# Adaptive layer norm, linear attention and SwiGLU on one core: key tiles in pairs, heads innermost, second-norm statistics by sums, and a new order

## The chip, the cores and the metric

The kernel runs on one core of one Trainium2 chip. The metric is the time of one execution on the device in microseconds (us). A core has five engines that run side by side, each through its own list of instructions in the order in which the program has them: TensorE (PE, matmuls, with its weight loads PEld beside them), VectorE (DVE), ScalarE (ACT), GpSimd (POOL) and SyncE (SP), which only issues transfers. An engine stops at an instruction whose semaphores have not been raised, and whatever stands behind it on that engine stops too.

## The reference

`x` is 2048 tokens of 512 numbers in bf16. The reference, cut to what matters:

```
mod = silu(c) @ w_mod                    # six vectors of 512: sa, ca, ga, sb, cb, gb
h   = layernorm(x) * (1 + ca) + sa
q, k, v = split(h @ wqkv)                # 32 heads of 16
phi(t) = concat(softmax(t @ w_phi), softmax(-(t @ w_phi)))    # 32 features a head
kv  = sum over tokens of phi(k) v^T ;  z = sum over tokens of phi(k)
o   = (phi(q) kv) / (phi(q) z + 1e-6)
x   = x + ga * (o @ wo)
h   = layernorm(x) * (1 + cb) + sb
out = x + gb * ((silu(h @ w_gate) * (h @ w_up)) @ w_down)     # 1376 hidden numbers
```

## The kernel before

The 2048 tokens are 16 tiles of 128, four to a chunk of x. The stages, with the lines of the profile:

- **Start.** silu(c) times w_mod gives the first norm's scale and shift `modA` (L473, L478). w_phi is spread into blocks `BD` (L499, L502) and folded into the key and query weights by transposes, matmuls and casts (L519, L523, L530, L533), so that a key tile comes out of PE as k times w_phi at once. The first norms of x run beside this.
- **Key tiles** (`k_tile`): four matmuls of 512 columns for k (L619) and four for v (L623); two exponentials on ACT, of the value and of its negative (L634); their sums over each head on DVE (`S`, L640); 1/S on ACT as exp(-ln S) (L644, L645); v times 1/S on DVE into `va` (L650), and 1/S itself as 32 more columns of `va` (L652 to L654); the second feature half scaled on POOL (L657). `kv_tile` adds phi(k) times va into the accumulator `kv_ps` (L663).
- **Query tiles** (`q_tile`): four matmuls (L686), two exponentials (L690), sums (L694), a reciprocal (L696), a ratio (L697), a scale (L701), and a transposing transfer into `pT`.
- **Attention** (`attend_tile`): eight short matmuls of pT with `KVZ` into `kv_ps` (L824). The program has one such bank, so the next tile's matmuls wait until DVE has read this one's: a reciprocal of the denominators (L827) and the product `o` (L828).
- **Projection and second norm** (`project`): o transposed, times wo (L857), added to x on DVE (L860), statistics on DVE (L348, L349), the reciprocal standard deviation on POOL (L359 to L362), the normalized tile on ACT, POOL or DVE, its transpose by a transfer, and scale and shift `modB` (L878 to L882).
- **Feed-forward**: gate and up (L909), silu on ACT (L916), the product on DVE or on ACT and POOL (L919, L923, L925), down (L987), the last sums (L993 to L1001) and the transfers out (L1007). The last tile's output leaves in three pieces, of 256, 128 and 128 columns.

What stands where on an engine is decided ahead of time. Each operation is recorded with `pl.op`, with one or more engines that could do it; `ORDER` is a table of numbers, one for each operation, which picks the engine and the order; `Plan.run` gives each operation a planned start from built-in costs, and the engines' lists are the operations sorted by it. Where the plan leaves PE idle in the first 90 us, `fill` puts matmuls of a tile of ones into the list (L1054), whose results nobody reads. They are meant to keep PE at work, and take the time of any matmul of their width. Such a matmul writes into `kv_ps` or into the bank that the next real matmul will write:

```
            elif late:
                dst = kv_ps[:, 0, :] if o.news[0].tag == "four" else one_ps[o.news[0].slot]
```

Of the kernel before, what the change touches and what calls it, by code (L numbers as in the profile page):

```python
# [14 lines left out]
P = 128  # L15
# [20 lines left out]
def fm_size(m):  # L36
# [53 lines left out]
class Buf:  # L90
# [14 lines left out]
    def free_at(self):  # L105
        if self.keep:
            return None
        t = 0.0
        for u in self.users:
            if u.end is None:  # L110
                return None
# [982 lines left out]
```

## Time and profile before

| | before |
|---|---|
| runs | 199.42, 199.49, 199.85 us (median 199.49) |
| span of the profiled execution | 197.6 us; of the same execution no other time is given |
| busy share PE, DVE, ACT, POOL | 98%, 71%, 56%, 60% |
| granted TensorE clock | 1.00 of full speed in every stretch |
| first key matmul, start of the last matmul | 12.74 us, 194.12 us |

The profile is one execution; its span runs from the first instruction to the last event, and the timed runs are 1.9 us longer at the median. Busy time is what an engine spends in instructions; the chain is the work that ended last, followed backwards from the end.

### The profile page before, as it was taken

The numbers are of one execution on the slowest core, as the hardware profiler recorded it, in microseconds if no ns is written. First come the engines' busy times: TensorE is split into PE (matmuls) and PEld (weight loads), VectorE is DVE, ScalarE is ACT, GpSimd is POOL, SyncE is SP. The second block draws the span as 40 slices with busy tenths as digits, with TensorE's granted clock in tenths as the row PEclk, the third lists the DMA queues.
The fourth block names the chain that finished last, engine by engine and source line by source line (L and its number), as shares of the span: only waits on it lengthen the run. The fifth ranks groups of instructions, "written<-read, shape, count | busy, mean of one in ns | idle before, by whom it ended". The sixth has DMA issues, their size and how long they took to land.

```text
span 197.6 us, 4084 instructions
## 1 busy us (share of the span) xinstructions
PE 192.9 (98%) x1495; PEld 108.4 (55%) x1495; DVE 139.9 (71%) x272; ACT 111.6 (56%) x252; POOL 119.5 (60%) x198
## 2 busy tenths in 40 slices
PE   7999999999999999999999999999999999999993
PEld 2765555555754776886575554454445444444452
DVE  5999999999999999989868689384122421181653
ACT  2699999999769982665263625435723411235200
POOL 1459999999996669656757979406761004065310
PEclk9999999999999999999999999999999999999999
DMA  6997994999928672835377515400340020100202
GB/s 210 370 373 116 168 316 162 213 181 389 324 53 170 117 138 42 157 65 102 77 113 135 109 36 87 100 0 0 80 98 25 0 63 17 56 15 27 80 29 79
DMA packets 51142, 24.17 MB, mean 122 GB/s; under 512 B 42449, under 2 KB 47922, under 8 KB 51122
## 3 DMA queue, kind: packets, MB, share of 16 engines
q1 hardware_dynamic: 50976, 23.88, 50.0%
q8 instruction: 11, 0.18, 0.3%
q14 instruction: 9, 0.07, 0.1%
q10 hardware_dynamic: 146, 0.03, 0.1%
HBM read 11.58 MB, written 2.10 MB: 69 GB/s over the span
## 4 chain that ended last, share of the span: by engine, by line
PE 98%; DVE 0%; issue 0%
PE one_ps L909 35%; PE one_ps L987 19%; PE one_ps L857 7%; PE one_ps L623 7%; PE one_ps L619 7%; PE one_ps L686 7%; PE kv_ps L1054 4%; PE one_ps L955 3%; PE kv_ps L663 2%; PE kv_ps L824 2%; PE one_ps L530 1%; PE one_ps L473 1%; PE one_ps L414 1%; PE one_ps L519 0%; PE one_ps L722 0%; DVE ones L296 0%
## 5 line engine op out<-in xcount | busy, mean ns | idle before, releaser
L909 PE MATMUL one_ps<-hT,wgu_sb 128*128 128x512 bf16 (+2 forms) x480 | 75.7, 308 | 0.0
L909 PEld LDWEIGHTS <-wgu_sb 128*128 128x128 bf16 x480 | 40.3, 98 | 27.7
L916 ACT ACTIVATE sg<-one_ps 128x512 bf16<-128x512 f32 (+1 forms) x41 | 23.7, 588 | 41.8 <-PE one_ps L909 29.9
L925 POOL TENSOR_TENSOR gu<-usb,sg 128x512 bf16<-128x512 bf16 x19 | 21.8, 1151 | 39.7 <-ACT usb L923 19.9
L987 PE MATMUL one_ps<-wd_sb,gu 128*128 128x512 bf16 (+1 forms) x160 | 37.7, 372 | 0.0
L919 DVE TENSOR_TENSOR gu<-one_ps,sg 128x512 bf16<-128x512 f32 (+1 forms) x22 | 14.3, 652 | 21.1 <-PE one_ps L909 19.0
L987 PEld LDWEIGHTS <-gu 128*128 128x128 bf16 x180 | 16.6, 98 | 16.7
L997 DVE TENSOR_TENSOR fg<-one_ps,gab 128x512 bf16<-128x512 f32 (+1 forms) x16 | 10.5, 669 | 19.6 <-PE one_ps L987 19.4
L348 DVE BATCH_NORM_STATS2 st<-x_c 128x6 f32<-128x512 bf16 x32 | 21.0, 679 | 0.1
L640 DVE TENSOR_REDUCE S<-e 128x64 f32<-128x1024 bf16 x16 | 19.1, 1207 | 0.2
L694 DVE TENSOR_REDUCE Sq<-eq 128x64 f32<-128x1024 bf16 x16 | 19.0, 1201 | 0.0
L923 ACT CAST usb<-one_ps 128x512 bf16<-128x512 f32 x19 | 11.3, 594 | 13.5 <-PE one_ps L909 13.2
L690 ACT ACTIVATE eq<-one_ps 128x512 bf16<-128x512 f32 x32 | 17.3, 644 | 2.2 <-PE one_ps L686 2.2
L634 ACT ACTIVATE e<-one_ps 128x512 bf16<-128x512 f32 x32 | 16.9, 600 | 0.0
L657 POOL TENSOR_TENSOR e<-e,S 128x512 bf16<-128x512 bf16 x16 | 16.8, 1056 | 0.1
L857 PE MATMUL one_ps<-wo_sb,oT 128*128 128x512 bf16 x64 | 16.1, 379 | 0.0
L623 PE MATMUL one_ps<-wv,hT 128*128 128x512 bf16 x64 | 16.1, 379 | 0.0
L619 PE MATMUL one_ps<-wk,hT 128*128 128x512 bf16 x64 | 15.8, 379 | 0.0
L686 PE MATMUL one_ps<-wq,hT 128*128 128x512 bf16 x64 | 15.8, 379 | 0.0
L701 POOL TENSOR_TENSOR eq<-eq,Rq 128x512 bf16<-128x512 bf16 x13 | 14.2, 1096 | 0.5
L860 DVE TENSOR_TENSOR x_c<-x_c,one_ps 128x512 bf16<-128x512 bf16 x16 | 10.6, 674 | 4.5 <-PE one_ps L857 4.4
L880 ACT ACTIVATE hT<-raw,modB 128x256 bf16<-128x256 bf16 x16 | 8.9, 594 | 8.1 <-DMA raw<-xn 8.1
(120 smaller groups left out, 279.8 us busy)
## 6 DMA issues: line engine op xcount, KB each, us to landing
wmod_sb<-in_w_mod_dram SPq DMA_DIRECT2D x2, 1024.0 KB, 8.5
out_dram<-ot SPq DMA_DIRECT2D x15, 128.0 KB, 2.0
x_c<-in_A_x_dram SPq DMA_DIRECT2D x3, 512.0 KB, 6.7
wgu_sb<-in_B_w_up_dram SPq DMA_DIRECT2D x1, 1376.0 KB, 10.2
wgu_sb<-in_B_w_gate_dram SPq DMA_DIRECT2D x1, 1376.0 KB, 13.1
wd_sb<-in_B_w_down_dram SPq DMA_DIRECT2D x1, 1280.0 KB, 6.8
wk<-in_A_wqkv_dram SPq DMA_DIRECT2D x1, 512.0 KB, 4.9
wmod_sb<-in_w_mod_dram SPq DMA_DIRECT2D x1, 512.0 KB, 5.3
```

The costliest lines, as they stand in the source:

```text
L348: pl.op("DVE", r=reads, w=[st6], us=0.6, fn=lambda: nc.vector.bn_stats(st6()[:], src))
L619: nc.tensor.matmul(pk()[:], lhsT=hT[c_i][k][:, cols], rhs=Wk2[:, k, :], start=(k == 0), stop=(k == KD - 1))
L623: nc.tensor.matmul(v()[:], lhsT=hT[c_i][k][:, cols], rhs=wv_sb[:, k, :], start=(k == 0), stop=(k == KD - 1))
L640: pl.op("DVE", r=[e], w=[Ss], us=1.13, fn=lambda: nc.vector.tensor_reduce(Ss()[:].rearrange("p g s h -> p (g s h)"), e()[:].rearrange("p g ...
L686: nc.tensor.matmul(pq()[:], lhsT=hT[c_i][k][:, cols], rhs=Wq2[:, k, :], start=(k == 0), stop=(k == KD - 1))
L690: pl.op("ACT", r=[pq, btab], w=[be[sg]], us=0.48, fn=lambda sg=sg: nc.scalar.activation(eq[:, :, sg].rearrange("p g h f -> p g (h f)"), pq ...
L694: pl.op("DVE", r=be, w=[Sq], us=1.13, fn=lambda: nc.vector.tensor_reduce(Sq()[:].rearrange("p g s h -> p (g s h)"), eq[:].rearrange("p g s ...
L857: nc.tensor.matmul(a()[:], lhsT=oT()[:, j0 + j, :], rhs=wo_sb[:, j, :], start=(j == 0), stop=(j == KD - 1))
L909: nc.tensor.matmul(ps_()[0:fsz, q * n:(q + 1) * n], lhsT=wgu_sb[:, k, i, m * P:m * P + fsz], rhs=h2[k], start=(k == 0), stop=(k == KD - 1))
L916: pl.op("ACT", r=[g, btab], w=[sg], us=0.08 + 0.41 * L / CW, fn=lambda: nc.scalar.activation(sg()[0:fsz, 0:L], g()[0:fsz, 0:L], ACT.Silu))
L925: pl.op("POOL", r=[usb, sg], w=[gu], us=0.17 + 0.98 * L / CW, fn=lambda: nc.gpsimd.tensor_tensor(gu()[0:fsz, 0:L], usb()[0:fsz, 0:L], sg() ...
L987: nc.tensor.matmul(fp()[:], lhsT=b()[0:fsz, c0:c0 + P], rhs=wd_[0:fsz, m, wcs], start=(m == 0), stop=(m == FM - 1))
```

## The change

- **Key tiles in pairs.** The sums of two tiles go into one tile `S`; 1/S of both is one Ln and one Exp of 128 columns on ACT, and the Exp writes straight into the extra columns of `va`, which now holds both tiles. The copies L652 to L654 are gone, the ratio is made once for a pair (`rho`), and kv is accumulated two tiles at a time.
- **Heads innermost.** Features are stored as [16 features][4 heads] and not [4 heads][16 features]. A reduction then reads its 16 numbers with a step of four elements, and a scale is read as a contiguous run of four.
- **Second norm of tiles 2 to 15.** The addition to x becomes an instruction that also sums its output (after's L921), and ACT squares x with a sum (L924); six small operations on POOL for a pair (`rstd_sums`) replace three for each tile and 14 of the 32 BN_STATS with their BN_AGGR.
- **Start.** The silu of c is Exp, Ln, Exp on ACT and one product on DVE; w_phi's block is first copied out and then multiplied in two halves; the four casts of the folded key weights are all on ACT (two were on DVE).
- **End.** Of the last tile's three pieces the middle one leaves on ACT's queue, and no longer the last one.
- **The plan.** A released buffer is picked by its last use, GpSimd and certain DVE operations exclude each other by intervals, one transfer constant is 0.85 and not 1.1, and `ORDER` is another table.

```diff
@@ k_tile, k_pair
-        pl.op([("DVE", 0.46, lambda: nc.vector.reciprocal(R()[:], Ss()[:])), ("ACT", 0.47, fr)], r=[Ss], w=[R])
...
+    def k_pair(i0):
+        Ss, parts = bS[i0]
+        R = sb("kph", "R", [P, 2, G, 8], FP32)
+        va = Buf("va", lambda slot: va_t[slot])
+        def fr():
+            nc.scalar.activation(R()[:], Ss()[:], ACT.Ln)
+            nc.scalar.activation(va()[:, :, :, HG:HG + 8], R()[:], ACT.Exp, scale=-1.0)
...
-        pl.op("DVE", r=[e], w=[Ss], us=1.13, fn=lambda: nc.vector.tensor_reduce(
-            Ss()[:].rearrange("p g s h -> p (g s h)"), e()[:].rearrange("p g s h f -> p (g s h) f"), axis=AX.X, op=ALU.add))
+            Ss()[:, y].rearrange("p g (s h) -> p (g s) h", s=2), e()[:].rearrange("p g s f h -> p (g s) h f"), axis=AX.X, op=ALU.add))
...
@@ project, prepare
+        pl.op("DVE", r=[a, bx[n]], w=[bx[n], sums[r]] + ([mv] if r == 0 else []), us=0.68, fn=lambda: nc.vector.scalar_tensor_tensor(
+            xs, in0=a()[:], scalar=1.0, in1=xs, op0=ALU.mult, op1=ALU.add, accum_out=mv()[:, r, 0:1]))
+        pl.op("ACT", r=[bx[n], mv, sums[r]], w=[sums[r]] + xn2[2], us=0.62, fn=lambda: nc.scalar.activation(
+            xn2[1](), xs, ACT.Square, scale=D ** -0.5, accum_out=mv()[:, r, 1:2]))
...
@@ ffn_down
-            on_act = c1 == D and h == 1
+            on_act = c0 == D // 2 and c1 < D
```

The real matmuls are the same in number and width, 427,380 columns in all (the widths in PE's two lists added up). The fill matmuls are 27 with 11,780 columns before and 30 with 13,809 after. Ahead of the first key matmul they have 11,025 columns before and 12,075 after; 512 columns of real transposes that stood ahead of it now stand behind it.

What PE has at the first key matmuls (`one_ps` are PSUM banks, `hT` the normalized and transposed x, `xn` the normalized x). Before:

```order
L414 MATMUL one_ps_75<-ident_b,xn_326 128x128
...
L1054 MATMUL kv_ps<-ones 128x184
L619 LDWEIGHTS hT_0_144
L619 MATMUL one_ps_78<-wk,hT_0_144 128x512
L619 MATMUL one_ps_78<-wk,hT_1_145 128x512
L619 MATMUL one_ps_78<-wk,hT_2_146 128x512
```

After:

```order
L1122 MATMUL kv_ps<-ones 128x385
L652 MATMUL one_ps_76<-wk,hT_0_143 128x512
L652 MATMUL one_ps_76<-wk,hT_1_144 128x512
L440 MATMUL one_ps_75<-ident_b,xn_326 128x128
...
L652 MATMUL one_ps_78<-wk,hT_0_143 128x512
L652 MATMUL one_ps_78<-wk,hT_1_144 128x512
L1122 MATMUL kv_ps<-ones 128x512
L1122 MATMUL kv_ps<-ones 128x198
L652 MATMUL one_ps_78<-wk,hT_2_145 128x512
```

Four transposes (the L440 rows) and a second pair of fill matmuls now stand between the halves of the first key tiles.

What PE has at the fifth tile's attention (`pT` are its transposed query features). Before, two query tiles are followed by a pair of transposes and then the attention. After:

```order
L736 MATMUL one_ps_73<-wq,hT_2_153 128x512
L736 MATMUL one_ps_73<-wq,hT_3_154 128x512
L1122 LDWEIGHTS ones
L1122 MATMUL kv_ps<-ones 128x512 [waits DVE_49]
L1122 MATMUL kv_ps<-ones 128x512
L877 LDWEIGHTS pT_817 [waits DMAHW0_49]
L877 MATMUL kv_ps<-KVZ,pT_817 128x68
```

Two fill matmuls into `kv_ps` are new there; the first waits for DVE, which must have read the fourth tile's attention out of that bank.

What DVE has up to that read, in before:

```order
L828 TENSOR_TENSOR o_1135<-kv_ps,A_1125 128x512
L696 RECIPROCAL Rq_786<-Sq_700 128x32
L860 TENSOR_TENSOR x_c_79<-x_c_79,one_ps_77 128x512
L827 RECIPROCAL A_1086<-kv_ps 128x32
L828 TENSOR_TENSOR o_1135<-kv_ps,A_1086 128x512
L348 BN_STATS st_378<-x_c_79 128x6
L349 BN_AGGR ln_1174<-st_378 128x2
L696 RECIPROCAL Rq_870<-Sq_633 128x32
```

and after:

```order
L915 TENSOR_TENSOR x_c_79<-x_c_79,one_ps_76 128x512
L355 BN_STATS st_243<-x_c_79 128x6
L356 BN_AGGR ln_1153<-st_243 128x2
L746 RECIPROCAL Rs_722<-Sq_630 128x32
L746 RECIPROCAL Rs_887<-Sq_841 128x32
L748 TENSOR_TENSOR Rq_889<-Rs_722,Sq_630 128x32
L880 RECIPROCAL A_1091<-kv_ps 128x32
L881 TENSOR_TENSOR o_1062<-kv_ps,A_1091 128x512
```

The first tile's addition to x (L860, now L915) was followed directly by a read of the attention (L827, L828); now its statistics and three small query operations stand in between.

The end of DVE's list, before:

```order
L997 TENSOR_TENSOR fg_1727<-one_ps_75,gab 128x512
L993 TENSOR_TENSOR ot_2127<-one_ps_76,x_c_82 128x128
L1001 TENSOR_TENSOR ot_2164<-x_c_82,fg_1727 128x512
L993 TENSOR_TENSOR ot_1930<-one_ps_77,x_c_82 128x128
L1089 UNCONDITIONAL_BRANCH
```

and after:

```order
L1062 TENSOR_TENSOR ot_1730<-x_c_82,fg_1792 128x512
L1058 TENSOR_TENSOR fg_1646<-one_ps_73,gab 128x512
L1054 TENSOR_TENSOR ot_1929<-one_ps_77,x_c_82 128x128
L1062 TENSOR_TENSOR ot_1800<-x_c_82,fg_1646 128x512
L1157 UNCONDITIONAL_BRANCH
```

The last operation was a 128-column piece, sent on ACT's queue; now it is the 512-column sum of another tile, sent on SP's queue, and on PE that tile's down matmuls stand ahead of the last 11 matmuls of 128 columns.

## Rows read from the trace of the kernel before

**Rows 1.** The page, busy time, share of the span and instructions of each engine.

```profile
PE 192.9 (98%) x1495; PEld 108.4 (55%) x1495; DVE 139.9 (71%) x272; ACT 111.6 (56%) x252; POOL 119.5 (60%) x198
```

**Rows 2.** The page, chain of work that ended last, share by engine.

```profile
PE 98%; DVE 0%; issue 0%
```

**Rows 3.** Waits of PE: us in total, times, longest us.

```profile
PE kv_ps L1054 <- DVE ones L296: 1.4, 1, 1.4
```

**Rows 4.** Timeline of PE, start: start us, us, engine, line, operation, names, shapes, count.

```profile
11.37 1.54 PE L1054 MATMUL kv_ps<-ones 128*128 128x512 bf16 x7
12.74 2.75 PE L619 MATMUL one_ps<-wk,hT 128*128 128x512 bf16 x12
15.33 0.48 PE L1054 MATMUL kv_ps<-ones 128*128 128x512 bf16 x2
```

**Rows 5.** Windows: stretch, length, busy us (instructions) by engine, clock, DMA share, GB/s.

```profile
20.00:25.00 5.00, 5.00 (x43) 2.88 (x42) 5.00 (x8) 4.96 (x14) 5.00 (x10) 1.00 1.04 171
```

**Rows 6.** Instructions of PE by form: names, shape, count, busy us, mean ns, idle before.

```profile
L909 PE MATMUL one_ps<-hT,wgu_sb 128*128 128x512 bf16 x240 | 56.2, 379 | 0.0
...
L686 PE MATMUL one_ps<-wq,hT 128*128 128x512 bf16 x64 | 15.8, 379 | 0.0
```

**Rows 7.** Timeline of PE, first projection and the attentions around it.

```profile
58.60 1.03 PE L857 MATMUL one_ps<-wo_sb,oT 128*128 128x512 bf16 x4
59.46 0.42 PE L824 MATMUL kv_ps<-KVZ,pT 128*128 128x68 bf16 x8
59.72 2.75 PE L686 MATMUL one_ps<-wq,hT 128*128 128x512 bf16 x12
```

**Rows 8.** Timeline of DVE in the same stretch.

```profile
59.66 0.69 DVE L860 TENSOR_TENSOR x_c<-x_c,one_ps 128x512 bf16<-128x512 bf16 x1 [0.24 <-PE one_ps L857]
60.27 0.35 DVE L827 RECIPROCAL A<-kv_ps 128x32 f32<-128x32 f32 x1
60.65 0.69 DVE L828 TENSOR_TENSOR o<-kv_ps,A 128x512 bf16<-128x512 f32 x1
61.26 0.68 DVE L348 BATCH_NORM_STATS2 st<-x_c 128x6 f32<-128x512 bf16 x1
61.97 0.18 DVE L349 BATCH_NORM_AGGREGATE ln<-st 128x2 f32<-128x6 f32 x1
62.07 0.32 DVE L696 RECIPROCAL Rq<-Sq 128x32 f32<-128x32 f32 x1
62.31 1.16 DVE L694 TENSOR_REDUCE Sq<-eq 128x64 f32<-128x1024 bf16 x1
```

**Rows 9.** Timeline of PE, DVE and ACT's queue at the end.

```profile
192.72 0.38 PE L987 MATMUL one_ps<-wd_sb,gut 96*128 96x512 bf16 x1
...
193.14 0.69 DVE L997 TENSOR_TENSOR fg<-one_ps,gab 128x512 bf16<-128x512 f32 x1 [1.18 <-PE one_ps L987]
...
193.81 0.29 DVE L993 TENSOR_TENSOR ot<-one_ps,x_c 128x128 bf16<-128x128 f32 x1
194.02 0.42 DVE L1001 TENSOR_TENSOR ot<-x_c,fg 128x512 bf16<-128x512 bf16 x1
194.12 0.22 PE L987 MATMUL one_ps<-wdg,gut 96*128 96x128 bf16 x1
194.38 0.29 DVE L993 TENSOR_TENSOR ot<-one_ps,x_c 128x128 bf16<-128x128 f32 x1
194.70 0.38 ACTq L1007 DMA_DIRECT2D out_dram<-ot  x1
```

**Rows 10.** DMA issues: names, queue, count, KB each, median us from issue to landing.

```profile
out_dram<-ot SPq DMA_DIRECT2D x15, 128.0 KB, 2.0
...
out_dram<-ot ACTq DMA_DIRECT2D x1, 32.0 KB, 1.9
```

**Rows 11.** Instructions of DVE by form.

```profile
L694 DVE TENSOR_REDUCE Sq<-eq 128x64 f32<-128x1024 bf16 x16 | 19.0, 1201 | 0.0
...
L701 DVE TENSOR_TENSOR eq<-eq,Rq 128x512 bf16<-128x512 bf16 x3 | 2.9, 952 | 0.1
```

**Rows 12.** Instructions of ACT and of POOL by form.

```profile
L396 ACT ACTIVATE xn<-x_c,ln_nmr,ln_rstd 128x512 bf16<-128x512 bf16 x8 | 6.5, 808 | 0.6 <-POOL ln_nmr L362 0.6
...
L360 POOL TENSOR_TENSOR ln_rstd<-ln_neg,mhalf 128x1 f32<-128x1 f32 x16 | 9.0, 562 | 1.3
```

More of the change, by code (lines that the diff above doesn't have):

```diff
@@ L105, in free_at, with last_use @@
     def free_at(self):
-        if self.keep:
+        if self.keep or any(u.end is None for u in self.users):
             return None
[L108 to L111, printed above, removed]
-            t = max(t, u.end + Plan.HOP[u.eng])
-        return t
+        return max(u.end + Plan.HOP[u.eng] for u in self.users)
+    def last_use(self):
+        return max(u.place for u in self.users)
 class Op:
@@ L163, in room @@
             t = 0.0 if old is None else old.free_at()
-            if t is not None and (best is None or t < best[0]):
-                best = (t, i)
-        return best
+            key = -1 if old is None else old.last_use() if t is not None else None
+            if key is not None and (best is None or key < best[0]):
+                best = (key, t, i)
+        return best[1:]
     def run(self, fill):
@@ L170, in run @@
         live = {t: {} for t in self.slots}
+        held = {"POOL": [], "DVE*": []}
         free["XBAR"], dma, sent = self.queue, 0.0, list(self.sent)
-        for x in ORDER:
+        for place, x in enumerate(ORDER):
             o = self.ops[x // 4]
+            o.place = place
             o.alt = o.alts[x % 4]
@@ L176, in run @@
             o.start = max([o.at, free[o.eng]] + [p.end + (self.HOP if p.eng != o.eng else self.OWN)[p.eng] for p in o.preds])
-            if o.alt[0] == "DVE*":
-                o.start = max(o.start, free["POOL"])
             if o.eng == "XBAR" and len(sent) >= self.LANES:
@@ L183, in run @@
                 o.start = max(o.start, t)
+            star = o.alt[0] == "DVE*"
+            if star or o.eng == "POOL":
+                for s, e in held["POOL" if star else "DVE*"][-8:]:
+                    if o.start < e and o.start + o.alt[1] > s:
+                        o.start = e
             for b in o.news:
@@ L186, in run @@
             o.end = free[o.eng] = o.start + o.alt[1]
-            if o.alt[0] == "DVE*":
-                free["POOL"] = max(free["POOL"], o.end)
+            if star or o.eng == "POOL":
+                held[o.alt[0]].append((o.start, o.end))
             if o.eng == "XBAR" and o.kb > 0:
@@ L282 @@
     pools["modp"] = modp
+    prep_cm = tc.tile_pool(name="prep", bufs=1)
+    prep = pools["prep"] = prep_cm.__enter__()
+    WTq = prep.tile([P, KD, D], BF16, name="WT0")
     lastf = fm_size(FM - 1)
@@ L317 @@
     nc.gpsimd.memset(eps_t[:], LN_EPS)
+    one_t = const.tile([P, 1], FP32, name="one")
+    nc.gpsimd.memset(one_t[:], 1.0)
     nc.scalar.add_instruction(mybir.InstLoadActFuncSet(name=nc.get_next_instruction_name(), act_func_set_id=6,
@@ L321 @@
     gul_t = [const.tile([P, 2, P], BF16, name=f"gul{i}") for i in range(slots["gul"])]
-    va_t = [const.tile([P, G, NDW], BF16, name=f"va{i}") for i in range(slots["va"])]
-    bm4 = const.tile([P, HG], FP32, name="bm4")
-    bm4z = const.tile([P, 4], FP32, name="bm4z")
+    va_t = [const.tile([P, 2, G, NDW + 4], BF16, name=f"va{i}") for i in range(slots["va"])]
+    bm4 = const.tile([P, 4, DH], FP32, name="bm4")
     KVZ = attn.tile([P, G, NDW], BF16, name="KVZ")
@@ L501, with f_BD @@
     pl.op("PE", r=[bphi], w=[phx], us=0.42, fn=f_phx)
-    pl.op("DVE", r=[phx], w=[bBD], us=0.6, fn=lambda: nc.vector.tensor_tensor(
-        BD[:], phx()[:].rearrange("p (j f) -> p j f", f=DH).unsqueeze(2).to_broadcast([P, KD, 8, DH]),
-        bm128[:].unsqueeze(1).to_broadcast([P, KD, 8, DH]), op=ALU.mult))
+    phs = prep.tile([P, KD * DH], FP32, name="phs")
+    bphs = Buf()
+    pl.op([("ACT", 0.14, lambda: nc.scalar.copy(phs[:], phx()[:])), ("DVE", 0.13, lambda: nc.vector.tensor_copy(phs[:], phx()[:]))],
+          r=[phx], w=[bphs])
+    def f_BD(eng):
+        for g in range(2):
+            eng.tensor_tensor(
+                BD[:, :, g], phs[:].rearrange("p (j f) -> p j f", f=DH).unsqueeze(3).to_broadcast([P, KD, DH, 4]),
+                bm8[:, 4 * g:4 * g + 4].unsqueeze(1).unsqueeze(1).to_broadcast([P, KD, DH, 4]), op=ALU.mult)
+    pl.op([("DVE", 0.7, lambda: f_BD(nc.vector)), ("POOL", 1.2, lambda: f_BD(nc.gpsimd))], r=[bphs], w=[bBD])
     bmask = Buf()
@@ L508, in fold_phi @@
     def fold_phi(col0, W2, bW2, bw):
-        WTb = prep.tile([P, KD, D], BF16, name=f"WT{col0}")
+        WTb = prep.tile([P, KD, D], BF16, name=f"WT{col0}") if col0 else WTq
         for i in range(KD):
@@ L766 @@
                 later(wd_sb[0:lastf, FM - 1, :], B_w_down[(FM - 1) * P:F, :], bwd[-1:], 96)
-        if i >= 2:
+        if i >= 2 and i % 2 == 1:
+            kv_tile(i - 3)
             kv_tile(i - 2)
```

167 lines of the change are left out of this document (101 added, 66 removed), and 79 rows, old and new, of the table ORDER.

## The prediction

> **What bounds the kernel now.** I read the page first. PE is busy 98% of the span [rows 1], and the chain that ended last is PE almost from end to end [rows 2]. Such a share is an average and its ends are modelled, so I asked two sharper views. The waits of PE name a single one, 1.4 us for the first tile of ones at the very start [rows 3]. And the timeline gives start-to-start times: the twelve key matmuls from 12.74 to 15.33 are 2.59/12 = 0.216 us each, with weights, hT and banks all there in time [rows 4]; twelve query matmuls from 59.72 and four of the projection before them keep the same pace [rows 7]. PE therefore runs back to back from 12.74 to its last matmul at 194.12. From 15 to 50 us VectorE, ScalarE and GpSimd are full too, as the stretch from 20 to 25 shows [rows 5], yet PE does not slow there. So the time is three pieces: the way to 12.74, the dense stretch, and 197.6 - 194.1 = 3.4 us behind the last matmul.
>
> It follows what a change can be worth. The real columns are the same before and after, so the dense stretch can't shrink by work taken from the other engines. They matter only if they make PE wait. What can change the time is fill matmuls, new waits of PE, and the end.
>
> **The change part by part.** *Other engines, off the path.* All of these are priced at nothing, because PE is the cover. The pairs take 16 short Ln and Exp and 13 to 16 copies from ScalarE, GpSimd and VectorE; the sums take 14 statistics from VectorE and give ScalarE 14 squares, for which the rows have no price (from the 0.6 of its 512-column copies to the 0.81 of a normalization [rows 12]; I take 0.7, together 10 us). If this cover were gone, what PE waits for would be late by the one operation concerned, 0.3 to 1.2 us at a time. I laid the four lists of the new order out at the spacing of the old rows and found no stretch in which one of them gets fuller than before, except the places below.
>
> *Reductions with a step of four elements.* No row shows one. Below, they cost what they cost now, 1.20 us for 1024 elements [rows 11]; above, I use the dearest price per element that a VectorE row of this size has, 0.952 us for 512 [rows 11], which makes 1.9 us. I take 1.2, since the same number of elements is read and the row of the same operation is the nearest; the upper end is a rival below. The Trainium skill (Vector Engine (DVE) Microarchitecture Reference, section "Measured stream behaviour on trn2", the access granule) speaks against the change: a source whose neighbours in the stream do not lie next to each other in memory took 1.73 ns a column where a contiguous one took 1.05. By it a reduction would be 1.97 us by my estimate from that page, and the sum would gain 32 x 0.77 = 25 us. The Trainium skill (SBUF — State Buffer, the note on SBUF cachelines) says the contrary: two hits in a 16-byte line keep full speed, and a step of four bf16 elements gives two; by it the sum stays. No row of before shows which holds.
>
> *Front.* The fill matmuls ahead of the first key matmul grow from 11,025 to 12,075 columns, while 512 real columns move behind it. Taken up to the same amount of real work (the second half of the first two key tiles), the new list has 1,005 fill columns more. At the pace of rows 4 (seven fill matmuls from 11.37 to 12.74) that is at most 1,005/512 x 0.216 = 0.42 us. The lower end is 0, if PE would have waited there for data. Laying the new list out from the landings of the old trace gives 0.3; I take **+0.35**. The moves of silu(c), w_phi's block and the casts lie beside PE here; the nearest consumer (the first key exponentials) has about 0.3 us to spare, which is the price if that cover goes, once.
>
> *Middle, the fifth tile's attention.* Here the order puts two fill matmuls into `kv_ps`, and the first must wait until VectorE has read the fourth tile's attention. Count both engines from T, the moment PE goes on after the first projection. PE comes to the fill after four query matmuls, one attention and eight query matmuls: 0.86 + 0.26 + 1.73 = 2.85 us (four matmuls take 59.46 - 58.60, an attention 59.72 - 59.46, twelve matmuls 2.58 [rows 7]). VectorE starts the addition to x 0.20 after T (59.66 against 59.46 [rows 7, 8]). What follows now depends on it, step by step: addition to statistics 0.72, statistics to aggregate 0.71, aggregate to reciprocal 0.10, two reciprocals at 0.24, the small product, reciprocal to `o` 0.38, and `o` 0.69, all start to start in rows 8. The product has no row on VectorE; its ends are 0.10 (the step past the aggregate) and 0.35 (a reciprocal of that size), and I take 0.2. Sum: 0.20 + 0.72 + 0.71 + 0.10 + 0.48 + 0.20 + 0.38 + 0.69 = 3.48. PE waits 3.48 - 2.85, about 0.65 with the signal on the way. Then the two fill matmuls run, 0.43, before an attention whose own data were there: together **+1.08**. The wait's lower end is 0.15 (if the dependent steps overlap by 0.08 each, as independent ones do), its upper end 1.15 (if VectorE is still with the third tile's read at T + 0.2). Queued behind the fill on PE are the attention, transposes and two projections, and all that follows, since PE never has time to catch up.
>
> *End.* Count from L, the start of the last matmul. Before, VectorE took the last piece 0.26 after L (194.38 against 194.12) and ACT's queue got it at L + 0.58; it takes 1.9 to land and the span ends another 1.0 after that: L + 3.4 [rows 9, 10]. After, the 512-column tile that ends 0.77 before L (one of its 512-column matmuls and ten of 128 lie between) is multiplied from L - 0.35 (VectorE follows a 512-column last matmul by 193.14 - 192.72 = 0.42), the 128-column piece comes next at about L + 0.3, and only then the 512-column sum, from L + 0.53 to L + 0.95 (0.42 [rows 9]). Its 128 KB leave at L + 1.06 and land in 2.0 [rows 10]; with the same 1.0 the span ends at L + 4.0. I take **+0.5**; the ends are +0.1 (this transfer as fast as the small one, and the sum right behind its product) and +0.8.
>
> *Sum.* 0.35 + 1.08 + 0.5 = 1.93, on a span of 197.6: 199.5. The profiled execution has no time but its span; the median of the runs is 1.9 above it (199.49 to 197.6), so **201.4 us**.
>
> **The rivals.** *The middle is hidden.* If VectorE's chain there overlaps, or its addition to x starts earlier, the wait is gone and only the two fill matmuls remain, or not even they: 0.85 to 1.3 in all, 200.3 to 200.8. Speaking for it: 0.65 is the difference of two sums of 3 us. Against: each step of the new order needs the result of the one before. It decides when VectorE is through at T + 2.85.
>
> *A further wait behind the middle.* The second norm's chain of a pair gets longer: a square of 0.6 to 0.8 where statistics of 0.68 + 0.18 stood, and six POOL operations in a row where three were (the power takes 0.56 [rows 12], the others about 0.25). Twice a wait of 0.5 to 0.8 on the normalized tile makes 202.4 to 203. Against it: from a projection to the first gate matmul that needs it the order has over 10 us of other matmuls.
>
> *Strided reductions cost 1.9 us.* 0.7 more on each of 32, in stretches where VectorE is full [rows 5]: 22 us, 221 to 223. The trace has nothing for it and nothing against it but that the number of elements read is the same. The Trainium skill (Vector Engine (DVE) Microarchitecture Reference, "Measured stream behaviour on trn2") would have it so, with its 25 us.
>
> *Faster, because the key and query stretch is not PE's after all.* If the records hide waits of PE there, relieving VectorE and ScalarE gives time back. The price: 15.8/64 = 0.247 us for a query matmul against 56.2/240 = 0.234 for a gate matmul [rows 6], 0.0127 x 192 = 2.4 us; with all three losses 199.0, with front and end alone 197.9. It decides if four matmuls of 512 in that stretch take more than 0.87. Against it: they take 0.86 in rows 4 and 7, and these shares differ by what else shares the time. *No change:* fill in the front replaces waiting, the middle is hidden and the small end of the last term holds, 199.5.
>
> **How the numbers follow.** Forecast 0.42 (200.9 to 201.9); middle hidden 0.20; further wait 0.15; strided reductions 0.06; faster 0.09; no change 0.08. A difference of 0.2% is 0.4 us, about the spread of the three runs, so faster means below 199.1 and slower above 199.9. Faster 0.09, same 0.08, slower 0.83. The range, 200.1 to 203.0, takes in the first three cases (0.77) and the near edge of no change; what it leaves out are the strided reductions and the other side.
>
> **What would show it.** Right: PE's waits name VectorE's `o` before a fill matmul near 64 us with about 0.65; the first key matmul at 12.8 to 12.9 and the dense stretch from there still at 0.86 for four; the last event 3.9 to 4.0 behind the last matmul's start; reductions at 1.2. Wrong: no such wait (200.3 to 200.8), a wait of PE for hT behind 70 us (202.4 and up), reductions of 1.5 or more, or a key stretch whose matmuls come closer together than before.

## The result, and the profile after

The changed kernel is slower: 201.09 us at the median (four runs, 200.55 to 201.91) against 199.67 for the kernel before beside it, a ratio of 1.0083 [1.0054, 1.0112]. Six more executions (the first experiment) gave 201.44 against 199.35, 1.0111 [1.0086, 1.0135]. That is an extra 1.1 to 2.7 us, where 1.93 were forecast.

The profiled execution of after took 200.55 us, the lowest of the four. Its page answers to [rows 1], the busy time of each engine, and below it the chain by engine, which answers to [rows 2].

```profile
PE 193.3 (97%) x1498; PEld 108.6 (55%) x1498; DVE 132.2 (67%) x271; ACT 112.9 (57%) x243; POOL 117.6 (59%) x184
...
PE 91%; DVE 5%; DMA 2%; issue 0%; DVEq 0%; SPq 0%
```

VectorE has lost 7.7 us of work, GpSimd 1.9, ScalarE has gained 1.3, and the span has grown by 1.06 us (197.56 to 198.62). The chain has changed its character: 5% of it now lies on VectorE. The waits of PE say where:

```profile
PE kv_ps L1122 <- DVE ones L304: 1.4, 1, 1.4
PE kv_ps L1122 <- DVE o L881: 0.3, 1, 0.3
```

The second row is new against [rows 3]: a fill matmul waits for VectorE's read of the attention. To see what it is worth, I compared the two traces at equal work: the time at which PE has done so many real columns (fill left out), after minus before, at points ahead of which the same matmuls lie in both. "After again" is the first experiment's execution:

```
real columns   115,000  130,000  200,000  426,000     (15,660: the front)
time in before    61.2     67.8     97.9    193.6
after            -0.12    +0.96    +0.90    +0.78     (-0.14)
after again      +0.91    +1.99    +1.91    +1.79     (+0.90)
```

So there are three pieces. The front was 0.14 *early* in this execution (0.90 late in the other). In the middle, between 61 and 68 us, both lose the same 1.08. From there on nothing is lost, and 0.1 to 0.2 comes back where before had a wait of its own (0.19 us for `oT` near 70 us). The last piece lies behind the last matmul, which starts at 194.90: 3.72 us to the end of the span, where before took 3.44. -0.14 + 1.08 - 0.16 + 0.28 = 1.06.

The timeline of PE through the middle, start, length, engine, line, operation, with the idle time ahead of it in brackets; it answers to [rows 7]:

```profile
60.46 1.02 PE L910 MATMUL one_ps<-wo_sb,oT 128*128 128x512 bf16 x4
61.51 1.02 PE L736 MATMUL one_ps<-wq,hT 128*128 128x512 bf16 x4
62.37 0.42 PE L877 MATMUL kv_ps<-KVZ,pT 128*128 128x68 bf16 x8
62.63 1.89 PE L736 MATMUL one_ps<-wq,hT 128*128 128x512 bf16 x8
64.78 0.59 PE L1122 MATMUL kv_ps<-ones 128*128 128x512 bf16 x2 [0.26 <-DVE o L881]
65.21 0.41 PE L877 MATMUL kv_ps<-KVZ,pT 128*128 128x68 bf16 x8
65.53 0.40 PE L440 MATMUL one_ps<-ident_b,xn 128*128 128x128 bf16 x4
```

And VectorE's beside it, which answers to [rows 8]:

```profile
61.62 0.68 DVE L915 TENSOR_TENSOR x_c<-x_c,one_ps 128x512 bf16<-128x512 bf16 x1
62.33 0.69 DVE L355 BATCH_NORM_STATS2 st<-x_c 128x6 f32<-128x512 bf16 x1
63.06 0.18 DVE L356 BATCH_NORM_AGGREGATE ln<-st 128x2 f32<-128x6 f32 x1
63.16 0.53 DVE L746 RECIPROCAL Rs<-Sq 128x32 f32<-128x32 f32 x2
63.61 0.13 DVE L748 TENSOR_TENSOR Rq<-Rs,Sq 128x32 bf16<-128x32 f32 x1
63.66 0.34 DVE L880 RECIPROCAL A<-kv_ps 128x32 f32<-128x32 f32 x1
64.03 0.69 DVE L881 TENSOR_TENSOR o<-kv_ps,A 128x512 bf16<-128x512 f32 x1
```

The chain of the prediction is there, step by step. It is easy to stop here, and the experiments show that one must not: the four transposes behind the attention (L440) read the first tile's normalized x, and GpSimd gets to that only now:

```profile
63.34 0.23 POOL L366 TENSOR_SCALAR ln_neg<-ln 128x1 f32<-128x1 f32 x1 [1.59 <-DVE ln L356]
63.66 0.58 POOL L367 TENSOR_TENSOR ln_rstd<-ln_neg,mhalf 128x1 f32<-128x1 f32 x1
64.34 0.26 POOL L369 TENSOR_SCALAR ln_nmr<-ln,ln_rstd 128x1 f32<-128x1 f32 x1
64.70 0.77 POOL L424 TENSOR_SCALAR xn<-x_c,ln_rstd,ln_nmr 128x512 bf16<-128x512 bf16 x1
```

`xn` is ready at 65.47, the transposes start at 65.53. Without the fill and its wait PE would have stood there at about 64.6 and waited all the same, a wait that the view does not show because something else delays PE first. Two smaller gaps are in no row of it either: after's PE loses 0.19 just ahead of 61.51, between the projection and the next query matmul, and before's lost 0.15 just ahead of its first-tile transposes at 64.44. Both are inside the 1.08.

The prices by form, names and shapes, count, busy us and mean ns, of VectorE (the first answers to [rows 11]):

```profile
L744 DVE TENSOR_REDUCE Sq<-eq 128x64 f32<-128x1024 bf16 x16 | 19.1, 1201 | 0.0
L675 DVE TENSOR_REDUCE S<-e 128x64 f32<-128x1024 bf16 x16 | 18.6, 1200 | 0.4 <-ACT e L667 0.4
...
L921 DVE SCALAR_TENSOR_TENSOR x_c<-one_ps,x_c 128x512 bf16<-128x512 f32 x14 | 9.3, 681 | 2.3 <-PE one_ps L910 2.1 <-ACT hT L448 0.2
...
L921 DVE DVE_READ_ACCUMULATOR x_c<-one_ps,x_c 128x1 f32 x14 | 1.1, 82 | 0.0
...
L752 DVE TENSOR_TENSOR eq<-eq,Rq 128x512 bf16<-128x512 bf16 x2 | 0.8, 416 | 0.0
```

The reduction with a step of four costs what it cost, 1.20 us. The scale takes VectorE 0.416 where it took 0.952 [rows 11]. Two things differ there: the heads are innermost, and the scale `Rq` is now in bf16 where it was in f32, which the list of changes does not name; no run tells them apart. The end, PE and VectorE and the queues, answers to [rows 9]:

```profile
194.54 0.69 DVE L1058 TENSOR_TENSOR fg<-one_ps,gab 128x512 bf16<-128x512 f32 x1 [0.37 <-PE one_ps L1048]
...
194.90 0.22 PE L1048 MATMUL one_ps<-wdg,gut 96*128 96x128 bf16 x1
195.16 0.29 DVE L1054 TENSOR_TENSOR ot<-one_ps,x_c 128x128 bf16<-128x128 f32 x1
195.37 0.42 DVE L1062 TENSOR_TENSOR ot<-x_c,fg 128x512 bf16<-128x512 bf16 x1
```

### The profile page after: what moved, and what is told of

Read it like the earlier page. It is cut to its first block, busy times and chain, and to the rows that moved or that the text cites. A ratio compares the mean times of both kernels' runs of the same rounds, so it can differ in the third digit from the quotient of the medians.

```text
span 198.6 us, 4047 instructions
## 1 busy us (share of the span) xinstructions
PE 193.3 (97%) x1498; PEld 108.6 (55%) x1498; DVE 132.2 (67%) x271; ACT 112.9 (57%) x243; POOL 117.6 (59%) x184
## 4 chain that ended last, share of the span: by engine, by line
PE 91%; DVE 5%; DMA 2%; issue 0%; DVEq 0%; SPq 0%
PE one_ps L970 35%; PE one_ps L1048 19%; PE one_ps L656 7%; PE one_ps L652 7%; PE one_ps L910 7%; PE one_ps L736 4%; PE one_ps L1016 3%; DMA wk<-in_A_wqkv_dram 2%; PE kv_ps L713 2%; PE kv_ps L1122 2%; PE kv_ps L877 2%; DVE o L881 1%; DVE Sq L744 1%; PE one_ps L563 1%; PE one_ps L499 1%; PE one_ps L440 1%
## 5 line engine op out<-in xcount | busy, mean ns | idle before, releaser
L675 DVE TENSOR_REDUCE S<-e 128x64 f32<-128x1024 bf16 x16 | 18.6, 1200 | 0.4 <-ACT e L667 0.4
L1062 POOL TENSOR_TENSOR ot<-x_c,fg 128x512 bf16<-128x512 bf16 x6 | 6.9, 1154 | 17.1 <-DVE fg L1058 9.6
L707 POOL TENSOR_TENSOR e<-e,rho 128x512 bf16<-128x512 bf16 x16 | 16.6, 1050 | 0.6 <-PE one_ps L656 0.2
L652 PE MATMUL one_ps<-wk,hT 128*128 128x512 bf16 x64 | 15.6, 379 | 0.0
L656 PE MATMUL one_ps<-wv,hT 128*128 128x512 bf16 x64 | 15.3, 379 | 0.0
L752 POOL TENSOR_TENSOR eq<-eq,Rq 128x512 bf16<-128x512 bf16 x14 | 14.7, 1051 | 0.5
L355 DVE BATCH_NORM_STATS2 st<-x_c 128x6 f32<-128x512 bf16 x18 | 11.5, 677 | 1.3 <-DMA x_c<-in_A_x_dram 1.3
L881 DVE TENSOR_TENSOR o<-kv_ps,A 128x512 bf16<-128x512 f32 x16 | 10.8, 677 | 0.4
```

The source lines that it names most:

```text
L652: nc.tensor.matmul(pk()[:], lhsT=hT[c_i][k][:, cols], rhs=Wk2[:, k, :], start=(k == 0), stop=(k == KD - 1))
L656: nc.tensor.matmul(v()[:], lhsT=hT[c_i][k][:, cols], rhs=wv_sb[:, k, :], start=(k == 0), stop=(k == KD - 1))
L675: pl.op("DVE", r=[e], w=([Ss] if y == 0 else []) + [parts[y]], us=1.13, fn=lambda: nc.vector.tensor_reduce(Ss()[:, y].rearrange("p g (s h) ...
```

## The experiments

The theories: **A**, the prediction's, that the middle costs the wait for VectorE's read and the fill behind it; without them it would be gone. **B**, that the order brings PE to the first tile's transposes too early, so that taking either away only moves the wait. The expectations name more rivals where they are put. Runs sent together stood beside the same runs of before.

**Again.** The changed kernel unchanged, five rounds (`e1_after_again`).

> The changed kernel as it is, for a second profile. Its four runs were 200.55 to 201.91 us, and the profiled one was the fastest. In it TensorE's clock rose at 4.7 us, within the fill matmuls, and the way to the first key matmul took 12.40 us, where the old kernel's profile had the rise behind 6 us and 12.74. Theory F (the front's fill counts, and the early clock hid it): in a profile whose clock rises behind 6 us the first key matmul starts at 12.8 to 12.9 and the span is 199.0 to 199.4. Rival (the front's fill replaces waiting): the first key matmul starts at 12.4 to 12.5 whenever the clock rises, and the spread comes from elsewhere. Time 200.9 to 201.3 by both.

Measured 201.44 us (200.68 to 202.48), 1.0111 [1.0086, 1.0135]; the profiled execution 201.52. The middle is the same 1.08, the end the same, but the first key matmul starts at 13.44, not 12.40. That 1.04 us is no difference of the kernels. Up to 6 us the program does the same in both; here is PE in after's profiled execution:

```profile
3.44 2.19 PE L1122 MATMUL kv_ps<-ones 128*128 128x512 bf16 x7
...
6.34 0.83 PE L552 MATMUL one_ps<-ident_b,wk 128*128 128x128 bf16 x12
```

The same view and the same matmuls in the execution profiled here:

```profile
3.45 2.99 PE L1122 MATMUL kv_ps<-ones 128*128 128x512 bf16 x7
...
7.13 1.07 PE L552 MATMUL one_ps<-ident_b,wk 128*128 128x128 bf16 x12
```

The fill matmuls of 512 columns follow one another at 0.427 us at first, which is 512 columns at 1.2 GHz, and at 0.216 later, which is 2.4 (the fast spacing, below). In the first trace that happens at 4.70 us, after the same fill matmuls from 1.4 us on. In the second it happens at about 7.7, among the twelve transposes that start at 7.13: the second to the sixth are still 0.107 us apart, the last six 0.056. (An expectation below takes 7.13 for that date, which is only where those transposes start. The column of the granted clock reads 1.00 in both; only the spacing shows it.) Over the fourteen profiled executions here, of kernels of both orders, it lay between 4.70 and about 7.7. With after's list at the start the first key matmul tends to come later with it: 12.40 at 4.70, 12.38 and 12.52 at 5.1, 12.81 at 6.0, 13.44 at 7.7. This is most of the difference between the profiled executions' fronts.

**No fill in the middle** (`e2_no_mid_fill`). Fill is planned up to 50 us only.

```diff
-FILL_FROM, FILL_TO, FILL = 1.3, 90.0, 0.85
+FILL_FROM, FILL_TO, FILL = 1.3, 50.0, 0.85
```

> The two fill matmuls ahead of the fifth tile's attention are left out, all else as in the changed kernel. Theory A, that of the prediction (PE waits for the read of kv_ps, and the fill's 0.43 us follow on the path): 0.43 us less, about 200.65, and the transposes of the first tile's second norm start at 65.1. Rival B (what sets the time there is the first tile's second norm, whose normalized tile is there at 65.47 in the profile, 0.06 before its transposes start): no change within 0.1 us; PE's wait moves from the fill to those transposes, about 0.4 us there.

Measured 201.00 us, 1.0083 [1.0067, 1.0098]. PE's timeline at the place:

```profile
65.83 0.41 PE L877 MATMUL kv_ps<-KVZ,pT 128*128 128x68 bf16 x8 [0.26 <-DVE o L881]
66.58 0.40 PE L440 MATMUL one_ps<-ident_b,xn 128*128 128x128 bf16 x4 [0.33 <-POOL xn L424]
```

The fill's 0.43 is gone and a wait for `xn` of the same size has come; at equal work the middle still costs 1.09 (+0.93 to +2.02). A falls, B holds. This execution (201.74, the slowest of its six) had also lost 0.95 near 32 us, ahead of the place: ScalarE waited 1.07 for a transfer into `raw` and PE then 0.56 for ScalarE. The traces of after, e1, e3, e4, e6 and e9 have no such wait, so it is not counted to the edit.

**The read first, and no fill** (`e3_read_first_no_fill`). VectorE reads the attention (A and `o`) before the two reciprocals and the product of the query tiles.

```diff
-FILL_FROM, FILL_TO, FILL = 1.3, 90.0, 0.85
+FILL_FROM, FILL_TO, FILL = 1.3, 50.0, 0.85
...
-    1592, 1080, 2280, 1112, 1564, 1620, 1628, 1624, 1300, 1304, 1308, 1085, 2284, 2288,
+    1592, 2280, 1564, 1620, 1628, 1624, 1300, 1304, 1308, 2284, 2288, 1080, 1112, 1085,
```

> As e2, and VectorE reads the fourth tile's attention ahead of the three small query operations (two reciprocals, one product) and not behind them. Theory A: the read ends 0.6 us earlier, PE does not wait for it, and with the fill gone the time is 0.85 us less than the changed kernel's, about 200.25. Rival B: no change, since statistics and normalization of the first tile stand where they stood; PE waits 0.8 us for the normalized tile.

Measured 201.02 us, 1.0086 [1.0070, 1.0101]. Both of A's items are away, and one wait has taken their place, whole:

```profile
65.93 0.40 PE L440 MATMUL one_ps<-ident_b,xn 128*128 128x128 bf16 x4 [0.75 <-POOL xn L424]
```

At equal work +0.29 becomes +1.37: 1.08 once more.

**The end with the pieces last** (`e4_tail_pieces_last`). The first 128-column piece (3752 to 3768) moves behind the other tiles, and the 512-column product and sum (3677, 3680) ahead of the last one.

```diff
-    3664, 3668, 3672, 3732, 3736, 3740, 3744, 3748, 3677, 3680,
+    3664, 3668, 3672, 3752, 3756, 3760, 3764, 3732, 3736, 3740, 3677, 3680, 3768, 3744, 3748,
```

> In the changed kernel's list the two 128-column pieces of the last tile both come last on PE, as before, and the 512-column tile ahead of them, so that VectorE's last operation is a 128-column piece again. Theory (the end costs what VectorE and the last large transfer do behind PE's last matmul, 3.70 us against 3.44 before): 0.25 us less, the span ending 3.4 to 3.5 behind the last matmul's start. Rival (the end is set by the queue of transfers out, whatever comes last): no change.

Measured 200.90 us (200.53 to 202.88), 1.0091 [1.0058, 1.0125], too coarse for what was at stake. The trace: the span ends 3.54 behind the last matmul's start, 0.17 less than after's, not 0.25, since the last piece now waits for its buffer, which a transfer still reads:

```profile
195.42 0.22 PE L1048 MATMUL one_ps<-wdg,gut 96*128 96x128 bf16 x1
...
196.16 0.29 DVE L1054 TENSOR_TENSOR ot<-one_ps,x_c 128x128 bf16<-128x128 f32 x1 [0.48 <-DMA out_dram<-ot]
```

**Before again** (`b1_before_again`), one execution, unchanged.

> The kernel before as it is, for a second profile. In five profiles of the changed kernel and its variants the start of the first key matmul follows the moment at which TensorE's granted clock rose: rise at 4.70, 5.13, 5.95, 5.98, 7.13 us gave 12.40, 12.52, 12.76, 12.81, 13.44. The first profile of the kernel before had the rise at about 6.3 and 12.74. Theory F (the list of matmuls sets the front in both kernels): here too the start moves by about 0.45 us for each us of the rise. Rival (before, other waits set the front): it stays at 12.6 to 12.8 wherever the clock rises.

199.70 us. The transposes from 6.99 us on are at the fast spacing, those up to 6.53 are not; in the first trace it changed at 6.3. The first key matmul starts at 12.89, 0.15 later than there. So the front of before moves with that date too.

**Two fill matmuls in before** (`e5_before_two_fills`), ahead of the attention at 62.3 us.

```diff
-            fns += [lambda: f(n)] * int((o.start - t0 - 0.1) * FILL / each)
+            fns += [lambda: f(n)] * (2 if o.n == 607 else int((o.start - t0 - 0.1) * FILL / each))
```

> The kernel before with the two 512-column fill matmuls put ahead of the fifth tile's attention, as the changed kernel has them. Theory (a fill matmul costs its 0.43 us where nothing else is waited for, and in the kernel before the normalized tile is there in time): 0.43 us more, about 199.8 beside 199.4, and the transposes of the first tile start 0.4 later without a wait. Rival (fill is taken back by waits further on): no change.

Twelve runs, 199.51 us, 0.9999 [0.9980, 1.0019]. In the trace the place costs 0.44 (+0.40 to +0.84 at equal work), just what two matmuls take; 0.2 comes back at 70 us, where the wait for `oT` disappears. What is left, 0.2 to 0.3, can't be seen in the times: the theory holds at the place, and not for the whole. The +0.40 ahead of the place is the front: the fast spacing came at 7.5 us here, and the first key matmul at 13.15.

**The front with less fill** (`e6_front_fill_as_before`), 1,095 columns fewer in the first key tiles' stretch; in after.

```diff
-            left = int((o.start - t0) * (1200 if t0 < 7.0 else 2400))
+            left = int((o.start - t0) * (1200 if t0 < 7.0 else 2400)) - {108: 710, 126: 295}.get(o.n, 0)
```

> The changed kernel with 1,095 columns of fill less in the front: the last of the five fill matmuls ahead of the first key matmul (385 columns) and the two behind it (710) are left out. Theory F (the fill stands on the path): 0.3 to 0.45 us less, about 200.7 to 200.9, and at the same rise of the clock the key and value matmuls reach the same work 0.3 to 0.45 earlier, less where hT is then waited for (it had 0.19 to spare with the earliest rise). Rival (the fill replaces waiting): no change; PE waits for hT instead.

201.27 us, 1.0093 [1.0070, 1.0117]. The first key matmul starts at 12.50, with the fast spacing from about 5.7, and a wait has come, `PE one_ps L652 <- ACT hT L599: 0.2` in the waits of PE: in after the third quarter of the first hT is ready at 13.59 and not at 12.37, behind four casts of the folded weights and two pieces of another tile on ScalarE (two casts and none before). Between e2 (0.02 early at 5.1) and e4 (0.22 late at 5.9) after's front would be at +0.1 to +0.2 there, an estimate; here it is at -0.01. So 1,095 columns, which take 0.46 us, were worth 0.1 to 0.2: with the fast spacing this early the fill mostly hides a wait for hT, and the rival is nearer than the theory.

**Less fill in before's front** (`e7_before_less_front_fill`), 2,048 columns.

```diff
-            left = int((o.start - t0) * (1200 if t0 < 7.0 else 2400))
+            left = int((o.start - t0) * (1200 if t0 < 7.0 else 2400)) - {106: 2048}.get(o.n, 0)
```

> The kernel before with 2,048 columns of fill less ahead of its first key matmul (0.86 us at full clock); its hT stood ready 1.0 us before it was read. Theory F (fill on the path): first key matmul at 11.9 instead of 12.74, and the time 0.5 to 0.85 us less, about 198.7, which would be faster than both kernels. Rival G (it is given back): between 15 and 50 us VectorE and ScalarE are full, so PE runs ahead and then waits for banks there; the lead is gone by 50 us, no change within 0.2.

Twelve runs, 199.57 us, 1.0010 [0.9987, 1.0033]. The first key matmul starts at 12.11, after a new wait for hT (the second row). At equal work the lead over before is 0.62 us at 17 us, 0.44 from 27 to 68, 0.20 at 98, and -0.05 at 140: spent at a value matmul near 22 us, on a longer wait for `oT` (the third row) and on one for a pT near 105 us. Not all of the 0.62 is the fill's: the fast spacing came at about 4.9 here and at 6.3 in before. e8, with the same list up to there, and b1 were both fast by 6.99; between these two the lead at 17 us is 0.30.

```profile
PE kv_ps L1054 <- DVE ones L296: 1.4, 1, 1.4
PE one_ps L619 <- DVE hT L567: 0.4, 1, 0.4
PE one_ps L857 <- DMA oT<-o: 0.3, 1, 0.3
```

The rival that has the lead given back is right, though that happens later than it said.

**The lead and two moved steps in before** (`e8_before_moved`): e7's front, a projection's matmuls and an attention placed a few steps later, no fill from 50 us.

```diff
-    1436, 2512, 2444, 2237, 2024, 2214, 1960, 1976, 1968,
+    1436, 2512, 2237, 2024, 2214, 1960, 1976, 2444, 1968,
...
-    2664, 3444, 1801, 2112, 2080, 2704, 3448,
+    2664, 1801, 2112, 2080, 2704, 3444, 3448,
```

> The kernel before with 2,048 columns of fill less in the front (as e7, where 0.62 us were won and given back in three places: 0.18 to 0.22 at a value matmul near 22 us, 0.24 at a projection that waits for o's transposing transfer near 70 us, 0.24 at an attention that waits for pT near 104 us), and with these two late ones moved: the projection behind the next transposes and gate matmuls, the attention behind the next four gate and up matmuls; fill only up to 50 us. Theory G (a lead of PE is given back where a transfer or another engine has a date of its own, and kept where the order has other matmuls to put there): 0.4 to 0.5 us faster than the kernel before. Rival (the lead meets the next such date further on, or the moved steps are late for theirs): no change within 0.2.

Twelve runs, 199.44 us against 199.73, 0.9988 [0.9974, 1.0002]: not told from no change. The profiled execution had only 0.15 of lead over before's first trace. The wait for `oT` is gone, and the same projection waits 0.51 for a bank that ScalarE still reads (`PE one_ps L857 <- ACT sg L916: 0.4`).

**No second-norm statistics for the first tile** (`x1_no_stats_tile0`). In after without the middle's fill; the first tile is normalized with constants, its statistics and POOL's three operations are left out, so its normalized values differ.

```diff
-            stats(lambda: mv()[:, 0, :], xs, [bx[n]], [mv])
-            bn, rstd_t, nmr_t = rstd_of(mv, 1, [mv], "ln2", slots["ln2"])
+            stats(lambda: mv()[:, 0, :], xs, [bx[n]], [mv], n == 0)
+            bn, rstd_t, nmr_t = rstd_of(mv, 1, [mv], "ln2", slots["ln2"], n == 0)
```

> The changed kernel without the two fill matmuls, and with the first tile's second-norm statistics and reciprocal standard deviation left out (two VectorE and three GpSimd operations; the tile is normalized with constants, so its outputs differ). Its normalized tile is then there about 2 us earlier, and VectorE's read of the fourth attention 0.9 earlier. Theory B alone (the norm chain is what sets the time there): the whole 0.92 us of the middle is gone, PE's waits from 60 to 68 us sum to under 0.2, about 200.1. Rival C (a third chain ends right behind it: ScalarE, busy with query exponentials without a break until 66.07, makes the first tile's hT, which is there at 67.39 and 67.73 and is read 0.21 and 0.05 later): PE's wait moves on to the first gate matmuls, 0.5 to 0.8 us there, and the gain is under 0.3.

200.97 us, 1.0068 [1.0047, 1.0088]: by the ratios 0.3 us under e2, within the intervals, where B alone had 0.9. The wait for `xn` is gone, and the first gate matmuls, which read the tile's hT, come 0.20 to 0.29 us too far apart four times (1.04 in all, from 66.7 to 68.0; this trace lacks some 25 matmul records, so the sum is rough). ScalarE tells why:

```profile
61.60 5.09 ACT L740 ACTIVATE eq<-one_ps 128x512 bf16<-128x512 f32 x10
66.38 1.66 ACT L448 ACTIVATE hT<-one_ps,modB 128x128 bf16<-128x128 bf16 x4
```

Ten query exponentials without a pause, and only then the four pieces of hT. It is a third date, just behind `xn`.

**The same, with two exponentials behind hT** (`x2_no_stats_exps_later`); the statistics are left out as in the last one.

```diff
-    1624, 1300, 1304, 1308, 1085, 2284,
+    1624, 1300, 1085, 2284,
...
-    1784, 1788, 1560,
+    1784, 1788, 1304, 1308, 1560,
```

> As x1 (no fill in the middle, the first tile's second-norm statistics left out), and ScalarE does the last query tile's two exponentials behind the first tile's four hT copies and not ahead of them. Theory C (in x1 PE waited 1.0 us at the first gate matmuls for ScalarE): hT is there 0.96 us earlier, PE's waits between 60 and 69 us sum to under 0.4, and the time is 0.7 to 0.9 us under x1's, about 200.1 to 200.3. Rival (ScalarE is behind with all of its query work, and the moved exponentials stop PE or VectorE right after): the wait moves on once more, under 0.3 us gained.

201.30 us, 1.0092 [1.0067, 1.0116]. The middle is gone up to the first gate matmuls (+0.39 at 61 us, +0.41 at 65), and is paid again further on, +1.03 at 68 and +1.66 at 98. Its waits of PE:

```profile
PE kv_ps L1122 <- DVE ones L304: 1.4, 1, 1.4
PE one_ps L970 <- ACT hT L941: 0.6, 1, 0.6
PE kv_ps L877 <- DMA pT<-eq: 0.4, 1, 0.4
```

The third row is the sixth tile's attention at 68.45, a fourth date; the second is a gate matmul at 78.7. The rival's price was right, its reason was not shown: that pT's transfer was issued at 65.01, before the moved exponentials ran (from 67.00), so they do not feed it. PE only came sooner to a date that stood. Whether they delay the hT of the second row I did not follow.

**Mended** (`e9_after_mended`), with nothing left out: no fill in the middle, the read first, the two exponentials later, the first tile normalized on VectorE (op 443: 1774 becomes 1772, behind the read), and e4's end.

```diff
-    1764, 1768, 1774, 1028,
+    1764, 1768, 1028,
...
-    1592, 1080, 2280, 1112, 1564, 1620, 1628, 1624, 1300, 1304, 1308, 1085, 2284, 2288,
+    1592, 2280, 1564, 1620, 1628, 1624, 1300, 2284, 2288, 1080, 1112, 1085, 1772,
```

> The changed kernel with nothing left out and all found dates moved earlier at once: no fill in the middle; VectorE reads the fourth attention ahead of the three query operations; VectorE normalizes the first tile (0.41 us) in place of GpSimd (0.77); ScalarE does the last two query exponentials behind hT; and the last tile's pieces come last as in e4. Theory (three chains end within 0.5 us of each other at this place, and all must be earlier): the normalized tile is there 0.3 to 0.4 earlier, the middle costs 0.4 to 0.6 and not 0.92, the end 0.15 less; together 0.5 to 0.7 under the changed kernel, about 200.5 where that is at 201.2. Rival: yet another date stands there, and only the end's 0.15 is won.

200.73 us (200.04 to 200.87), 1.0059 [1.0037, 1.0080]. The middle costs 0.54 (-0.15 to +0.39), half of what it did, and the waits name one that remains:

```profile
65.08 0.40 PE L440 MATMUL one_ps<-ident_b,xn 128*128 128x128 bf16 x4 [0.34 <-DVE xn L418]
```

Its front is within 0.02 us of after's first trace, and its span 0.50 shorter (198.12 against 198.62), the low end of what was expected; it is still slower than before. No version tried beats before by more than can be measured.

## Why the prediction was right, and where it was not

**Direction and size.** The forecast of +1.93 held within the interval (1.1 to 2.7 us in two sets of runs). It stood on the reading that PE has no idle time to win back. That is nearly so: before's PE lost 0.15 ahead of 64.44 and 0.19 near 70.6, and taking fill away (e7, e8) won nothing that can be measured. In after, nothing more is lost from 68 us to the last matmul, so the accumulated sums, squares and small POOL operations cost and gain nothing there.

**Middle: right in place and size, wrong in what the price belongs to.** The forecast was 1.08, and 1.07 to 1.09 is what after, its repeat and e2, e3, e4 and e6 lose between 61 and 68 us. The steps of the sum were close: T is 61.51, VectorE goes on at T + 0.11 (0.20 was taken), reads `o` from T + 2.52 and lets the fill start at T + 3.27, where 3.48 stood. The largest miss is the small product, 0.05 and not 0.2. (The 0.72 from addition to statistics is not in rows 8, where the read of the attention lies between; it measured 0.71.) The wait is so 0.42, not 0.65, with 0.43 of fill behind it. The rest are 0.07 at the transposes, 0.13 at the first gate matmuls and 0.19 ahead of T, less the 0.15 that before lost at the place. The last four were not in the forecast, so that both sums come to about 1.08 is luck.

The step that failed is the clause that the fill runs "before an attention whose own data were there". The attention's were; those of the transposes behind it were not, so that fill and wait are cover for a later date. The rival of a further wait was set aside because the order has "over 10 us of other matmuls" from a projection to its gate matmul; for the first tile it has 6.0 (61.51 to 67.49), and 4.0 to the transposes.

The account that e2 and e3 leave is a shorter sum. From the projection's end to the transposes PE has 20 query matmuls and two attentions in before (59.46 to 64.44, 4.98 us, 0.15 of it a wait), but 12 and two in after, which at the spacing of rows 7 are 0.86 + 0.26 + 1.73 + 0.26 = 3.11 us. The first tile's addition, statistics, POOL's three steps and `xn` take from 61.51 to 65.53, 4.02 us. 4.02 - 3.11 = 0.91, whatever stands in between; with 0.13 for hT, 0.19 ahead of T and before's 0.15 taken off it is 1.08. Eight query matmuls have gone ahead of the projection, which itself stands 1.86 later (60.46 against 58.60). The last of the four scalings of wo on GpSimd ends at 60.41 (57.05 before), and the projection takes all four, so it could not have been earlier; why they are later is open, and an order with earlier scalings was not tried.

**The relief was real, and had nowhere to go.** VectorE runs that chain 0.96 sooner than before, since its read of the attention no longer stands between addition and statistics. But of ScalarE's relief in the key stretch the middle got nothing. (Over the whole span ScalarE has none: 111.6 us of work before, 112.9 after, with the squares.) Windows of after, with the busy time of PE, PEld, DVE, ACT and POOL:

```profile
45.00:50.00 5.00, 5.00 (x38) 2.49 (x36) 4.97 (x7) 3.54 (x9) 4.53 (x8) 1.00 1.03 116
50.00:55.00 5.00, 5.00 (x69) 3.23 (x67) 5.00 (x9) 2.13 (x6) 4.78 (x6) 1.00 1.03 305
55.00:60.00 5.00, 5.00 (x43) 2.64 (x40) 4.99 (x10) 3.25 (x7) 5.00 (x6) 1.00 0.46 69
60.00:65.00 5.00, 4.71 (x39) 2.36 (x38) 4.86 (x12) 5.00 (x11) 3.04 (x7) 1.00 0.68 130
```

ScalarE is idle for 6.1 of the 15 us up to 60 (3.3 in before) and has not a moment left in the five behind (nor had it in before), where the exponentials stand in a row ahead of hT. The longest of its waits there, 2.15 us up to 55.96, is for PE's query matmuls, and so are three more, of 0.27 to 0.52: the order brings them late. That the first dates lie one behind another (VectorE's read, `xn`, hT, the sixth pT) is shown by e3, x1 and x2: each one taken away puts PE before the next, at the same price in e3 (1.08), at about that in x1, and in x2 at 0.64 by 68 us and 0.63 more by 98. That this is why before is hard to beat is not shown; only e7 and e8 speak to it.

**Front: +0.35 was of the right order, and not a constant.** The date of the fast spacing moves it from -0.14 (4.70 us) to +0.90 (about 7.7). At 6.3, the date in the first trace of before, after would be at about +0.4, an estimate between e3 (6.0, +0.27) and the repeat. The late dates agree: e5 has before's front and was 0.40 late with the spacing at 7.5, the repeat 0.90 at 7.7, a difference of 0.5, of which some 0.1, an estimate, is the later date. With it 0.4 + 1.08 - 0.16 + 0.28 = 1.6, inside the measured interval. At the early dates the fill hides a wait for hT (e6), so the term is smaller there.

**End: mis-sized.** +0.28, not +0.5. The product started at L - 0.36 as forecast, the piece at L + 0.26, the sum at L + 0.47 (0.53 forecast), its transfer at L + 0.91 (1.06) and it landed in about 1.8 (2.0): the end is L + 3.72, not L + 4.0.

**The rivals.** *Middle hidden* and *no change* did not happen. *A further wait behind the middle* did not add to the sum, yet its kind, a wait for the normalized tile, is what e2 and e3 laid open. *Faster* falls: the four groups of 512 columns keep 0.86 to 0.87. *Strided reductions* fall, at 1.200 us for a step of four. The Trainium skill (Vector Engine (DVE) Microarchitecture Reference, "Measured stream behaviour on trn2") made 1.97 of it by my estimate, from a row for 4-byte elements that hop 4 KiB each; the estimate does not hold for this shape. The Trainium skill (SBUF — State Buffer, the note on SBUF cachelines) agrees with the trace.

## What to carry to other kernels

A wait that the profile names can be the first of several: before it is priced, count the slack to each consumer that stands behind it, since taking away fill, a wait or a producer moves the price and does not lower it until all the dates behind are earlier too. An engine that is relieved gives nothing to a bound engine unless what it makes is due earlier; here the order spent the relief on idle time in one stretch and on haste in the next. Compare two traces at equal real work, not at equal time: the same 1.07 to 1.09 us in six profiles says more here than medians that differ by 0.5.

## What the runs showed of the hardware that was not expected

- The same list of instructions at the start had its 512-column matmuls at 0.427 us up to 4.70 us in one execution, and matmuls of that slower pace up to about 7.7 in another, with 0.216 from there on. With fill up to the first key tile, its start moved with that from 12.40 to 13.44 and the execution by nearly as much (200.55 to 201.52).
- A reduction of 1024 bf16 elements with a step of four is as fast as with a step of one: 1.200 and 1.201 us, where [rows 11] have 1.201.
- An output that is summed on the way has an instruction of its own for reading the sum: 0.082 us on VectorE behind an addition of 0.681, 0.221 on ScalarE behind a square of 0.652.
